# A ConvNeXt-V2 block on one core: squares ahead of norms, bn_stats of half means, and one convolution bank in three copied by VectorE in some slots

## The chip, the cores and the metric

The kernel runs on one core of one Trainium2 chip. A core has a matrix engine (TensorE, PE in the profile, with its weight loads as PEld), VectorE (DVE), ScalarE (ACT), GpSimd (POOL) and SyncE (SP, used here to issue DMA transfers). Each engine works through its own queue in order; semaphores hold an instruction until what it needs is there. TensorE writes into PSUM (8 banks of 128 partitions by 512 f32 values); the other tiles lie in SBUF; DRAM is reached by DMA. The metric is device time of the whole program in microseconds (us), smaller is better.

## The reference

The input is one image of 512 x 512 pixels with C = 96 channels in bf16; the hidden width is 4C = 384.

```python
for i in range(K):                       # K = 3: depthwise 3 x 3 convolution
    for j in range(K):
        out = out + xp[:, i:i+H, j:j+W, :] * dw[i, j][None, None, None, :]
h = _layernorm(out, axis=-1)             # over the 96 channels of a pixel, eps 1e-5
h = jnp.einsum('bhwc,ce->bhwe', h, w1)   # 96 -> 384
h = _gelu(h)
gx = jnp.sqrt((h * h).sum(axis=(1, 2), keepdims=True) + 1e-6)   # per channel, over all pixels
nx = gx / (gx.mean(axis=-1, keepdims=True) + 1e-6)
h = grn_gamma * (h * nx) + grn_beta + h
h = jnp.einsum('bhwe,ec->bhwc', h, w2)   # 384 -> 96
return x + h
```

The sum of h * h per channel needs every pixel before the second product can be scaled. So there are two phases: all pixels through convolution, norm, first product and GELU for the sums, and then all pixels again through the second product.

## The kernel before

The image is cut into 128 blocks of four rows (2048 pixels each). **Phase 1** is a loop over slots (line 832 on); slot s works on many blocks at once, each at its own stage. A table `at` says which stage of which block falls into which slot. For a block b in the steady part: its x rows are loaded by SP four slots ahead (`load_x`), turned by two VectorE transposes in slot b - 3 (`turn_x`), and convolved on TensorE in slot b (`conv_taps`), in three bursts of 24 matmuls into three PSUM banks, Y3. Each burst uses two of the banks: the first banks 0 and 1, the second 1 and 2, the third 2 and 0. `evac` (line 500) writes the three banks to the bf16 tile `y_bf` with one ScalarE instruction. In slot b + 1 GpSimd squares it (`stage_sq`, tile `ysq`); in slot b + 2 TensorE sums y and y^2 over channels (`stage_stats`, matmuls with `rowsel`), VectorE moves the sums of four blocks out of PSUM (`stage_moments`, tile `mom`), and over the next slots GpSimd makes 1/sigma of the four blocks (`stage_rstd` and `stage_newton`), VectorE transposes it (`rt`), SP writes it to DRAM and reads it back spread over partitions (`rbc`, about four slots later). In slot b + 10 GpSimd multiplies (`stage_norm`, tile `yn`), in b + 11 SP writes yn to DRAM and in b + 12 reads it back with channels on partitions (`ynT`), and in b + 14 the block goes through the first product and GELU (`mlp_units`).

Such a slot with a product has twelve PSUM banks of product, each turned to `g` by ScalarE's GELU: three instructions of 1024 columns and six of 512. The order in a slot is written out by hand in lines 894 to 924: convolution bursts (`conv`), products (`unit`), g^2 statistics (`squares`) and the sums of y (`stage_stats`) take turns. At the top of the slot (lines 833 to 850) stand SP's issues and GpSimd's work: `newton`, then `norm` of block s - 10 (line 845), then the square of block s - 1 (line 847), then `rstd`. SP's issues follow the same order in every slot: the x load, the ynT read, the write of yn, `rbc` or the rows of 1/sigma, a third of a stored g.

**The sums of g^2.** A part of g (`cm_quads(b)` of its four quarters: 4 for a block that is stored whole, b mod 10 in 0, 3, 7; 2 for the block behind such a one; 3 for the rest) has channels on partitions, and VectorE takes `bn_stats` of each 512 values of a channel (`entry`, tile `bst`). `bn_stats` gives six numbers: count, mean and count times variance of one half of the values (256), and the same of the other half. The remaining quarters go through TensorE (`gram`). A whole block's last three statistics are put off to the end of the next slot, so each slot has nine. Each 32 entries make a group; `aggregate` (line 774) reduces a group with three `bn_aggr`, one for each 128 channels, to mean and variance (`mv`), and `second_moments` (line 784) turns them into sums of squares (`parts`): once for all groups but the last in the last slot but one, and once for the last group behind the last slot. The chain from there to the scaled weights `W2s` stands ahead of phase 2.

From slot 128 on there is no convolution (`mlp_tail`): a drain in which the last blocks wait for norms. **Phase 2** then goes over all blocks with g held, stored or recomputed (`gr`), and writes the output.

In set-up, `Wd` lies in one of the five `g` buffers, before its first use; `dwx` is a constant tile of its own, and `npx` holds the number of values of each group.

Of the kernel before, what the change touches and what calls it, by code (L numbers as in the profile page):

```python
# [56 lines left out]
def kernel(  # L57
# [80 lines left out]
    dwx = consts.tile([9, NI, GR, 32], bf16, name="dwx")  # L138
# [17 lines left out]
    mv = consts.tile([128, NCH, NACC, 2], f32, name="mv")  # L156
    parts = consts.tile([128, NCH, NACC + 1], f32, name="parts")
    npx = consts.tile([128, NACC], f32, name="npx")
    grp = {}
    NYT = 6  # L160
    yn_ring = [prepool.tile([128, GR, W], bf16, name=f"ynT{i}") for i in range(NYT)]
# [25 lines left out]
    with ExitStack() as p1:  # L187
# [31 lines left out]
        def load_x(b):  # L219
# [15 lines left out]
                sp.dma_start(out=o, in_=i_)  # L235
            xins[b] = t

        Wd = gpool.tile([128, NQ, NCH, QW], bf16, name="g")[:].rearrange("p t j w -> p (t j w)")[
            :, :NI * 9 * 32].rearrange("p (i k c) -> p i k c", i=NI, k=9)
# [163 lines left out]
        n = 0  # L403
# [35 lines left out]

        def setup_rest():  # L440
            dve.memset(ones_f[:], 1.0)
            for k in range(NACC):
                dve.memset(npx[:, k:k + 1], float(GROUPS[k] * QW))
            dve.tensor_copy(out=gam[:], in_=gam_bf[:])

        def turn_x(b):
# [20 lines left out]
        def conv_taps(b, spare):  # L467
            if spare:
                Ua, Ub = banks(2), banks(1)
                Y = [Ua[:, 0, :], Ua[:, 1, :], Ub[:, 0, :]]  # L470
            else:
                Y = [Y3[:, i, :] for i in range(NI)]
            mms = []
            for n in range(3):
                mms.append([(h, j, (n + h) % NI, dx) for dx in (0, -1, 1) for j in range(GR) for h in range(2)])
            flat = [m for ms in mms for m in ms]
            first = {}
            last = {}
            for n, (h, j, i, dx) in enumerate(flat):
                first.setdefault((i, j), n)  # L480
                last[i, j] = n

            def burst(n, fence=True):
                k = sum(len(ms) for ms in mms[:n])
                for h, j, i, dx in mms[n]:
                    src = b + shift(h, j)
                    o0, o1 = max(0, -dx), W - max(0, dx)
                    pe.matmul(
                        Y[i][32 * j:32 * j + 32, o0:o1],
                        lhsT=Wq[64 * h:64 * h + 64, i, dx + 1, j, :],  # L490
                        rhs=x_rows(src, 64 * h, 64 * h + 64, i, MB * (1 + dx) + o0, o1 - o0)
                        if 0 <= src < NBLK else zrow[64 * h:64 * h + 64, o0:o1],
                        start=first[i, j] == k,
                        stop=last[i, j] == k,
                    )
                    k += 1
                if n < 2 and fence:
                    pe.drain()

            def evac():  # L500
                y = ypool.tile([128, NI, W], bf16, name="y_bf")
                if spare:
                    act.activation(out=y[:, 0:2, :], in_=Ua, func=ACTF.Identity)
                    act.activation(out=y[:, 2, :], in_=Ub[:, 0, :], func=ACTF.Identity)
                else:
                    act.activation(out=y[:], in_=Y3, func=ACTF.Identity)
                ybf[b] = y
# [270 lines left out]

        def combine(b):
            for k in sorted(bsts):  # L780
# [49 lines left out]
        for s in range(last_slot + 1):  # L830
# [11 lines left out]
            store_next()  # L842
            for k in get("newton"):
                stage_newton(k, pool)
            for b in get("norm"):
                stage_norm(b)
            for b in get("sqp"):
                stage_sq(b, False)
            for k in get("rstd"):
                stage_rstd(k, pool)  # L850
            mlp = get("mlp")
# [37 lines left out]
            else:  # L889
# [25 lines left out]
                unit(8, 2)  # L915
                unit(10, 1)
# [30 lines left out]
            if s == last_slot - 2:  # L947
                for n in range(PRE):
                    load_xr(n, sp)
            if s == last_slot - 1:  # L950
                for n in range(3):
                    stage_xb(ORDER[n], pool, B2bc_f)
                second_moments(0, NACC - 1)
            if s == last_slot:
                for n in range(PRE):
                    load_rest(n, sp, sp)
# [8 lines left out]
        dve.tensor_reduce(out=sums[:], in_=parts[:, :, :NACC], axis=AX.X, op=ALU.add)  # L965
        for j in range(NCH):
            junk = bstpool.tile([128, 128], f32, name="junk")
            dve.scalar_tensor_tensor(out=junk[:], in0=gram[:, j, :], scalar=1.0, in1=ident_f[:],
                                     op0=ALU.mult, op1=ALU.mult, accum_out=parts[:, j, NACC:NACC + 1])
        ssq = gsm.tile([128, NCH], f32, name="ssq")  # L970
        dve.scalar_tensor_tensor(out=ssq[:], in0=sums[:], scalar=GRN_EPS, in1=parts[:, :, NACC],
                                 op0=ALU.add, op1=ALU.add)
        gi = gsm.tile([128, NCH], i32, name="gi")
        dve.tensor_scalar(out=gi[:], in0=ssq[:].bitcast(i32), scalar1=-0.5, scalar2=float(0x5F3759DF),
# [84 lines left out]
```

## Time and profile before

| what | us |
|---|---|
| median of three runs (1481.1, 1482.73, 1484.31) | 1482.73 |
| the profiled execution's own time | 1478.75 |
| its span from first to last instruction | 1477.0 |
| busy: TensorE, VectorE, ScalarE, GpSimd | 1392.1, 1182.9, 1413.9, 1300.8 |
| g^2 statistics on VectorE (`bst<-g`, 1110) | 671.1 |
| evictions of y_bf on ScalarE (135) | 199.9 |
| norms (126) and squares (114) on GpSimd | 391.2 and 313.7 |
| aggregates of a full group on VectorE (33) | 30.4 |

All instructions issued through the kernel's in-order wrapper carry line 35, so groups are told apart by their tiles: `y_bf<-PS` is the eviction of a convolution, `g<-PS` a GELU, `bst<-g` a statistic, `mv<-bst` an aggregate, `xT<-xin` a transpose, `ysq<-y_bf` a square, `yn<-y_bf,rbc` a norm, and `PS<-rowsel,ysq` the sums of y^2 on TensorE. A line of the timeline gives the start, the length, the engine, the operation, the tiles, the shape and the number of instructions that stand together, and in brackets the idle time ahead of it and what ended that. Phase 1 ends near 972 us.

### The profile page before, as it was taken

The page shows a single profiled execution, that of the slowest core. Times are in us where ns is not written, and L with a number is a line of the kernel's source. Part 1 is how long each engine was busy: PE and PEld are TensorE (multiplying, and loading weights), DVE is VectorE, ACT ScalarE, POOL GpSimd, SP SyncE. Part 2 cuts the span into 40 slices and gives each one's busy share as a digit, 9 for nine tenths or more (in the row PEclk, how much of TensorE's full clock was granted, in tenths as well). Part 3 has the DMA queues.
Part 4 walks back from the last instruction along what each step waited for, and adds up shares of the span by engine and source line. Part 5 has one row for each costly group of instructions (what it writes and reads, how often), then busy time and mean ns, then how long its engine had stood idle before and what let it go on. Part 6 is the DMA issues. An engine that isn't in the chain of part 4 may idle for free.

```text
span 1477.0 us, 54487 instructions
## 1 busy us (share of the span) xinstructions
PE 1392.1 (94%) x23125; PEld 811.5 (55%) x23125; DVE 1182.9 (80%) x2135; ACT 1413.9 (96%) x1595; POOL 1300.8 (88%) x923
## 2 busy tenths in 40 slices
PE   7888989999999999999999998789999999999998
PEld 3343444444444444444444445467777767777766
DVE  7748989999999999999999987965555555555545
ACT  6888989999999999999999999999999999999987
POOL 2559899999999999999989988569999999999997
PEclk9999999999999999999999999999999999999999
DMA  6577788888878888888878866659999999999997
GB/s 180 164 218 240 236 248 268 258 264 255 282 236 262 269 268 257 277 245 272 261 245 270 271 212 191 201 193 364 367 327 386 397 379 398 404 392 406 387 373 306
DMA packets 167913, 422.03 MB, mean 286 GB/s; under 512 B 34326, under 2 KB 84182, under 8 KB 163190
## 3 DMA queue, kind: packets, MB, share of 16 engines
q1 hardware_dynamic: 151428, 314.98, 65.0%
q0 software_dynamic: 14880, 103.43, 18.6%
q8 instruction: 181, 2.97, 0.9%
q14 instruction: 62, 0.51, 0.1%
q10 hardware_dynamic: 1362, 0.15, 0.1%
HBM read 262.16 MB, written 156.22 MB: 283 GB/s over the span
## 4 chain that ended last, share of the span: by engine, by line
PE 28%; ACT 23%; POOL 19%; DMA 17%; issue 5%; SPq 5%; DVE 3%; POOLq 0%; ACTq 0%; DVEq 0%
PE PS L35 28%; ACT g L35 16%; POOL yn L35 6%; POOL xb L327 6%; ACT y_bf L35 5%; SPq L35 5%; POOL ysq L35 4%; DMA ynT<-yn_dram 4%; DMA out_dram<-o_sb 3%; DMA yn_dram<-yn 3%; DMA rbc<-r_dram 3%; DMA xin<-in_x_dram 2%; DVE bst L35 1%; DMA g_dram<-g 1%; ACT gr L35 1%
## 5 line engine op out<-in xcount | busy, mean ns | idle before, releaser
L35 ACT ACTIVATE g<-PS 128x512 bf16<-128x512 f32 (+2 forms) x1062 | 727.9, 868 | 15.3 <-PE PS L35 15.0
L35 DVE BATCH_NORM_STATS2 bst<-g 128x6 f32<-128x512 bf16 x1110 | 671.1, 674 | 35.4 <-ACT g L35 34.8
L35 ACT ACTIVATE gr<-PS 128x1536 bf16<-128x1536 f32 x360 | 498.1, 1458 | 17.5 <-PE PS L35 13.1
L35 POOL TENSOR_TENSOR yn<-y_bf,rbc 128x1536 bf16<-128x1536 bf16 x126 | 391.2, 3107 | 78.3 <-ACT rbc L35 24.1
L35 DVE TENSOR_TENSOR o_sb<-PS,xb 128x384 bf16<-128x384 f32 x512 | 278.4, 557 | 224.2 <-PE PS L35 189.9
L327 POOL TENSOR_TENSOR xb<-xr,B2c 128x1536 f32<-128x1536 bf16 x118 | 368.2, 3135 | 2.0 <-POOL xb L327 0.5
L35 PE MATMUL PS<-xT,Wq 64*32 64x511 bf16 (+1 forms) x9198 | 340.5, 389 | 26.2 <-ACT y_bf L35 9.2
L35 PE MATMUL PS<-ynT,w1p 128*128 128x512 bf16 x1161 | 335.1, 383 | 25.0 <-ACT g L35 5.4
L35 POOL TENSOR_TENSOR ysq<-y_bf 128x1536 bf16<-128x1536 bf16 x114 | 313.7, 2752 | 12.8 <-ACT y_bf L35 12.8
L35 PE MATMUL PS<-ynT,w1s 128*128 128x512 bf16 x1020 | 276.3, 380 | 0.0
L35 PEld LDWEIGHTS <-gr 128*128 128x128 bf16 x4296 | 212.5, 98 | 64.0 <-issue 6.0
L35 PE MATMUL PS<-W2s,gr 128*128 128x96 bf16 x4224 | 223.7, 206 | 4.8 <-DVE o_sb L35 4.6
L35 PEld LDWEIGHTS <-Wq 64*32 64x32 bf16 x9216 | 111.9, 90 | 193.3 <-issue 144.7
L35 ACT ACTIVATE y_bf<-PS 128x1536 bf16<-128x1536 f32 (+2 forms) x135 | 199.9, 1486 | 16.6 <-PE PS L35 12.1
L35 PEld LDWEIGHTS <-w1p 128*128 128x128 bf16 x1161 | 89.7, 98 | 183.0 <-issue 128.6
L35 DVE STREAM_TRANSPOSE xT<-xin 128x576 f32<-128x576 f32 (+1 forms) x256 | 181.7, 750 | 7.8 <-DMA xin<-in_x_dram 7.7
L35 PEld LDWEIGHTS <-g 128*128 128x128 bf16 x1704 | 104.8, 98 | 86.7 <-issue 54.8
L35 PE MATMUL PS<-w1p,ynT 128*128 128x256 bf16 (+2 forms) x822 | 125.2, 272 | 7.8 <-ACT xT L35 3.2
L35 PE MATMUL PS<-g 128*128 128x128 bf16 x1464 | 122.6, 220 | 2.8 <-DVE PS L35 2.5
L35 PEld LDWEIGHTS <-w1s 128*128 128x128 bf16 x1020 | 82.2, 98 | 40.8 <-issue 0.6
L35 PEld LDWEIGHTS <-gl 128*128 128x128 bf16 x1680 | 83.4, 98 | 28.4 <-issue 7.0
L35 PE MATMUL PS<-W2s,gl 128*128 128x96 bf16 x1680 | 90.3, 206 | 4.2 <-DVE o_sb L35 3.9
(108 smaller groups left out, 704.3 us busy)
## 6 DMA issues: line engine op xcount, KB each, us to landing
xin<-in_x_dram SPq DMA_DIRECT2D x126, 432.0 KB
g_dram<-g SPq DMA_DIRECT2D x105, 512.0 KB
gl<-g_dram POOLq DMA_DIRECT2D x35, 1536.0 KB, 10.5
yn_dram<-yn SPq DMA_DIRECT2D x512, 96.0 KB
ynT<-yn_dram SPq DMA_DIRECT2D x128, 384.0 KB
out_dram<-o_sb SPq DMA_DIRECT2D x127, 384.0 KB
xr<-in_x_dram POOLq DMA_DIRECT2D x123, 384.0 KB, 6.6
ynT<-yn_dram SPq DMA_DIRECT2D x255, 128.0 KB
```

The lines of the kernel that those rows point to most:

```text
L35: r = f(*a, **k)
L327: pq.tensor_tensor(out=xb[:], in0=grp[q]["xr"][:], in1=bias[:, None, :].to_broadcast([128, PXP, C]), op=ALU.add)
```

## The change

In words, part by part:

- In each slot GpSimd makes the square (`sqp`) ahead of the norm.
- `aggregate` takes, for each 128 channels, one `bn_stats` of the group's half means (twice the number of entries, up to 64 values, 24 bytes apart), and one reduction that adds the half variances (times count) of all three. `second_moments` has five operations where it had three, and its early call comes one slot earlier.
- In slots with a convolution whose product block has `cm_quads` of 2, ScalarE evicts banks 0 and 1 of the convolution and VectorE copies bank 2; there the third pair of statistics, `squares(2)`, stands behind that copy in VectorE's queue.
- `dwx` moves into the `g` buffer that holds `Wd`; `npx` and its memsets go; the sums of `gram`'s diagonal get a tile of their own.

```diff
+    mom2 = consts.tile([128, NCH, NACC, 2, 3], f32, name="mom2")
+    tot2 = consts.tile([128, NACC, NCH], f32, name="tot2")
+    parts = consts.tile([128, NCH, NACC, 2], f32, name="parts")
...
-            def evac():
+            def evac(shared=False):
                 y = ypool.tile([128, NI, W], bf16, name="y_bf")
-                if spare:
+                if shared:
+                    act.activation(out=y[:, 0:2, :], in_=Y3[:, 0:2, :], func=ACTF.Identity)
+                    dve.tensor_copy(out=y[:, 2, :], in_=Y3[:, 2, :])
+                elif spare:
...
         def aggregate(k):
             bst = bsts.pop(k)
+            n = 2 * GROUPS[k]
+            v = bst[:].rearrange("p j e (h s) -> p j (e h) s", h=2)[:, :, :n]
             for j in range(NCH):
-                dve.bn_aggr(out=mv[:, j, k, :], in_=bst[:, j, :GROUPS[k], :].rearrange("p a s -> p (a s)"))
+                dve.bn_stats(out=mom2[:, j, k].rearrange("p h s -> p (h s)"), in_=v[:, j, :, 1])
+            dve.tensor_reduce(out=tot2[:, k, :], in_=v[:, :, :, 2], axis=AX.X, op=ALU.add)
...
         def second_moments(k0, k1):
-            v, p = mv[:, :, k0:k1, :], parts[:, :, k0:k1]
-            dve.tensor_tensor(out=p, in0=v[:, :, :, 0], in1=v[:, :, :, 0], op=ALU.mult)
-            dve.tensor_tensor(out=p, in0=p, in1=v[:, :, :, 1], op=ALU.add)
-            dve.tensor_tensor(out=p, in0=p, in1=npx[:, None, k0:k1].to_broadcast([128, NCH, k1 - k0]), op=ALU.mult)
+            v, p = mom2[:, :, k0:k1], parts[:, :, k0:k1]
+            dve.tensor_tensor(out=p, in0=v[:, :, :, :, 1], in1=v[:, :, :, :, 1], op=ALU.mult)
+            dve.tensor_tensor(out=p, in0=p, in1=v[:, :, :, :, 0], op=ALU.mult)
+            dve.tensor_tensor(out=p, in0=p, in1=v[:, :, :, :, 2], op=ALU.add)
+            dve.tensor_scalar(out=p, in0=p, scalar1=float(QW // 2), scalar2=None, op0=ALU.mult)
+            dve.tensor_tensor(out=p[:, :, :, 0], in0=p[:, :, :, 0],
+                              in1=tot2[:, k0:k1, :].rearrange("p k j -> p j k"), op=ALU.add)
...
+            for b in get("sqp"):
+                stage_sq(b, False)
             for b in get("norm"):
                 stage_norm(b)
-            for b in get("sqp"):
-                stage_sq(b, False)
...
+                shared = evac is not None and cm_quads(b) == 2
                 unit(6, 1)
-                squares(2)
+                if not shared:
+                    squares(2)
                 unit(7, 1)
...
                 conv(2)
                 if evac:
-                    evac()
+                    evac(shared)
+                if shared:
+                    squares(2)
```

More of the change, by code (lines that the diff above doesn't have):

```diff
@@ L137 @@
     dw9 = consts.tile([9, C], bf16, name="dw9")
-    dwx = consts.tile([9, NI, GR, 32], bf16, name="dwx")
     eye32 = consts.tile([128, 32], bf16, name="eye32")
@@ L155 @@
     NACC = len(GROUPS)
-    mv = consts.tile([128, NCH, NACC, 2], f32, name="mv")
-    parts = consts.tile([128, NCH, NACC + 1], f32, name="parts")
-    npx = consts.tile([128, NACC], f32, name="npx")
+    mom2 = consts.tile([128, NCH, NACC, 2, 3], f32, name="mom2")
+    tot2 = consts.tile([128, NACC, NCH], f32, name="tot2")
+    parts = consts.tile([128, NCH, NACC, 2], f32, name="parts")
+    dsum = consts.tile([128, NCH], f32, name="dsum")
     grp = {}
@@ L236, in load_x @@
             xins[b] = t
-        Wd = gpool.tile([128, NQ, NCH, QW], bf16, name="g")[:].rearrange("p t j w -> p (t j w)")[
-            :, :NI * 9 * 32].rearrange("p (i k c) -> p i k c", i=NI, k=9)
+        g_setup = gpool.tile([128, NQ, NCH, QW], bf16, name="g")[:].rearrange("p t j w -> p (t j w)")
+        Wd = g_setup[:, :NI * 9 * 32].rearrange("p (i k c) -> p i k c", i=NI, k=9)
+        dwx = g_setup[:9, NI * 9 * 32:NI * 9 * 32 + NI * GR * 32].rearrange("p (i q c) -> p i q c", i=NI, q=GR)
         zrow = consts.tile([128, W], bf16, name="zrow")
@@ L441, in setup_rest @@
             dve.memset(ones_f[:], 1.0)
-            for k in range(NACC):
-                dve.memset(npx[:, k:k + 1], float(GROUPS[k] * QW))
             dve.tensor_copy(out=gam[:], in_=gam_bf[:])
@@ L949 @@
                     load_xr(n, sp)
+                second_moments(0, NACC - 1)
             if s == last_slot - 1:
@@ L952 @@
                     stage_xb(ORDER[n], pool, B2bc_f)
-                second_moments(0, NACC - 1)
             if s == last_slot:
@@ L964 @@
         sums = gsm.tile([128, NCH], f32, name="sums")
-        dve.tensor_reduce(out=sums[:], in_=parts[:, :, :NACC], axis=AX.X, op=ALU.add)
+        dve.tensor_reduce(out=sums[:], in_=parts[:].rearrange("p j k h -> p j (k h)"), axis=AX.X, op=ALU.add)
         for j in range(NCH):
@@ L968 @@
             dve.scalar_tensor_tensor(out=junk[:], in0=gram[:, j, :], scalar=1.0, in1=ident_f[:],
-                                     op0=ALU.mult, op1=ALU.mult, accum_out=parts[:, j, NACC:NACC + 1])
+                                     op0=ALU.mult, op1=ALU.mult, accum_out=dsum[:, j:j + 1])
         ssq = gsm.tile([128, NCH], f32, name="ssq")
-        dve.scalar_tensor_tensor(out=ssq[:], in0=sums[:], scalar=GRN_EPS, in1=parts[:, :, NACC],
+        dve.scalar_tensor_tensor(out=ssq[:], in0=sums[:], scalar=GRN_EPS, in1=dsum[:],
                                  op0=ALU.add, op1=ALU.add)
```

## The prediction, before the changed kernel was run

> **What bounds the kernel now.** First the page's part on busy time in 40 slices (about 37 us each; slices 7 to 23 are the steady part of phase 1):
>
> ```profile
> DVE  7748989999999999999999987965555555555545
> ACT  6888989999999999999999999999999999999987
> POOL 2559899999999999999989988569999999999997
> ```
>
> All are full in phase 1. The busy time by stretch says how full (columns: stretch, its us, then busy us of PE, PEld, DVE, ACT and POOL):
>
> ```profile
> 100.00:127.00 27.00, 20.81 (x342) 9.13 (x340) 19.76 (x33) 21.48 (x32) 19.58 (x18) 0.94 0.78 226
> 241.00:840.00 599.00, 576.58 (x10461) 283.41 (x10459) 596.60 (x1024) 598.67 (x852) 564.61 (x422) 1.00 0.84 262
> 883.00:900.00 17.00, 12.48 (x146) 8.38 (x143) 11.16 (x21) 13.04 (x12) 16.26 (x15) 0.90 0.59 185
> ```
>
> From 241 to 840 us ScalarE (ACT) and VectorE (DVE) both lack under 0.5% of being always busy, and VectorE's row of waits for this stretch is empty. ScalarE loses time in two places only, near 117 and near 890. Next, a slot in order of time:
>
> ```profile
> 410.14 1.57 ACT L35 ACTIVATE y_bf<-PS 128x1536 bf16<-128x1536 f32 x1
> 411.48 1.65 ACT L35 ACTIVATE g<-PS 128x1024 bf16<-128x1024 f32 x2
> ...
> 410.36 1.42 DVE L35 STREAM_TRANSPOSE xT<-xin 128x576 f32<-128x576 f32 x2
> 411.70 5.40 DVE L35 BATCH_NORM_STATS2 bst<-g 128x6 f32<-128x512 bf16 x9
> 417.01 1.42 DVE L35 STREAM_TRANSPOSE xT<-xin 128x576 f32<-128x576 f32 x2
> ...
> 411.24 0.38 PE L35 MATMUL PS<-w1p,ynT 128*128 128x128 bf16 x2
> 411.77 0.87 PE L35 MATMUL PS<-xT,Wq 64*32 64x512 bf16 x24 [0.15 <-ACT y_bf L35]
> ...
> 308.99 2.77 DVE L35 BATCH_NORM_AGGREGATE mv<-bst 128x2 f32<-128x192 f32 x3
> 311.68 1.22 DVE L35 BATCH_NORM_STATS2 bst<-g 128x6 f32<-128x512 bf16 x2
> ```
>
> Starts count, since neighbours overlap by some 0.08 us on VectorE and 0.2 us on ScalarE. ScalarE: y_bf 1.34 us (410.14 to 411.48), and a slot of about 7.04. VectorE: two transposes 1.34, nine statistics 5.31 (411.70 to 417.01, 0.59 each), so about 6.65, 0.15 for moments, and 2.69 for three aggregates about every 10.7 slots: 7.05. TensorE's next convolution burst starts 0.15 us late, on y_bf. Last, the two stalls:
>
> ```profile
> 114.09 3.09 POOL L35 TENSOR_TENSOR yn<-y_bf,rbc 128x1536 bf16<-128x1536 bf16 x1
> 117.14 2.75 POOL L35 TENSOR_TENSOR ysq<-y_bf 128x1536 bf16<-128x1536 bf16 x1
> ...
> 119.94 0.46 PE L35 MATMUL PS<-rowsel,ysq 128*128 128x4 bf16 x12 [4.62 <-POOL ysq L35]
> 122.37 1.46 PE L35 MATMUL PS<-ynT,w1p 128*128 128x512 bf16 x3
> 124.57 0.82 PE L35 MATMUL PS<-ynT,w1p 128*128 128x512 bf16 x3
> ...
> 892.23 0.46 PE L35 MATMUL PS<-rowsel,ysq 128*128 128x4 bf16 x12 [2.23 <-POOL ysq L35]
> ```
>
> At both places TensorE stands still for a square that GpSimd (POOL) makes behind a norm.
>
> **Squares in front of norms.** GpSimd's work is the same; each square comes 3.05 us earlier (117.14 less 114.09), each norm 2.75 later. At 119.94 the wait falls from 4.62 to 1.57: -3.05 us, all on the path, since ScalarE idles there. Between 241 and 840 nothing waits long for squares: 0. At 892 up to -2.5 us (2.23, and 0.3 at 898) is to be had, but a later norm is queued in front of everything SP does: the write of yn waits for it, and behind the write stand the store of g, the reload of rbc, the next x load and the next ynT read. Cover: in the steady part ynT reads are issued 10 to 17 us ahead of use and land in about 5, and x loads land at least 3.4 us before their transposes, mostly 5 to 10; 2.75 fits. In the drain reads are issued about 8 us ahead and land in 3 to 5, so 2.75 and the 2.5 gained use up the 3 to 5 that are spare. I take -0.7 there (ends -2.5 and +1), and +0.5 for x loads that come late in the batches with least room (0 to +3).
>
> **Half means on VectorE.** Between 241 and 840 there are 25 aggregates at 0.90: 22.4 us go. In their place 25 bn_stats of 64 values and 8.3 reductions of 192. No row shows either. A statistic of 512 starts 0.59 before the next; 448 values less at 1.04 ns (a VectorE column: 557 ns at 384 columns of o_sb against 279 at 128 of mom is 1.09, 0.59 over 512 less a start-up is about 1) leaves 0.125; bounds 0.07 (a memset of 128) and 0.2. A reduction of 39 takes 0.19, so one of 192 some 0.35, started 0.27 before the next; bounds 0.1 and 0.9 (the aggregate that read the same 192). Sum 3.1 + 2.3 = 5.4 us, between 2.6 and 12.5.
>
> **A third of y_bf on VectorE.** By the schedule 35 slots share, 25 of them between 241 and 840. ScalarE saves 512 columns: 1.34 less the 0.90 that a 1024 takes, 0.43 us; TensorE passes on at most 0.3 of it, because its last unit (411.24 and 0.22 for two) leaves 411.46 as the earliest start of the burst that now begins at 411.77. The copy on VectorE is bounded by the cast of 512 f32 in SBUF (0.43 long, 0.35 apart) and by 557 ns scaled from 384 to 512 (0.74). Two o_sb additions in a row stand 0.51 apart, also out of PSUM; with 128 columns more that is 0.64, which I take, as the nearest row. 25 x 0.64 = 16 us, between 8.7 and 18.6.
>
> [...]
>
> VectorE's balance between 241 and 840: -22.4 + 5.4 + 16.0 = -1.0 us, with ends -11 and +9. ScalarE could give 25 x 0.3 = 7.5, but VectorE has no free time, and it may no longer fall behind: bank 2 of the convolution is needed by the next slot's second burst, some 3.1 us after y_bf begins, and the copy ends 3.2 us behind the transposes' start (1.34 transposes, 1.18 two squares, 0.68 copy). So VectorE paces this stretch, and -1.0 is what arrives. Behind the copy in VectorE's queue wait squares(2) and all later statistics; who waits for those is only the g buffers, slots away. In slots 17 to 27 VectorE has room (27% of 100:127 is idle): 4 x 0.3 = -1.2. In slot 6 VectorE is on the chain that leads to the first rstd: +0.6.
>
> **The rest.** Behind the last statistics three aggregates (0.57) become three small bn_stats and a reduction (about 0.4), and three dependent additions at 0.2 become five: +0.3, on the path to W2s. The earlier part of second_moments lies where VectorE waits for ScalarE; dwx in g and dropped memsets cost nothing, they are set-up. Phase 2 (505 us) is untouched.
>
> **Sum.** -3.05 - 0.7 + 0.5 - 1.0 - 1.2 + 0.6 + 0.3 = -4.5 us on the profiled 1478.75. That execution is 4.0 below the median of 1482.73; on the median, 1478.2.
>
> [...]
>
> **Rivals.** (1) The copy is cheap, 0.35: 7.2 us less on VectorE, until TensorE's 7.5 binds: 1471.7. For it: the cast's row; against: every PSUM row. Chance 0.10. (2) The drain pays in full and x loads are never late (-1.8 and -0.5): 1475.9. For it: GpSimd waits 2.66 us for rbc at 876, room for a square. 0.12. (3) Slower: VectorE's new work costs more than it frees. Place: the saturated stretch, where each 0.1 us on a copy is 2.5 us, and a stride of 24 bytes under the statistics has no row. At the upper ends +9 in place of -1.0: 1488. It decides from +3.5 on the balance (copy 0.82, or reduction 0.8), where the forecast's gain is gone. 0.25, of which 0.05 ends within 0.2%. (4) Later norms eat the gain: SP falls behind, x loads and ynT reads come late, and the 4.5 us are given back: 1482.7. 0.10, half same, half slower.
>
> **The numbers.** Forecast 0.43, own range 1474.5 to 1481.5. What a measurement tells from no change is 0.2%, 3 us: of the forecast 0.32 is faster, 0.11 same. Faster 0.32 + 0.10 + 0.12 = 0.54; same 0.11 + 0.05 + 0.05 = 0.21; slower 0.20 + 0.05 = 0.25. The range 1471 to 1488 leaves out the best part of (1) and the worst of (3), some 0.15.
>
> **What would show it.** The wait at 119.94 about 1.6; none at 892; VectorE's busy time between 241 and 840 still full, while ScalarE's falls by about 9 us with small idle pieces put down to PE; the copy 0.68 long. Wrong if VectorE begins to idle (rival 1), if its balance is over +3.5, or if transposes wait for x or TensorE for ynT.

## The result and the profile after

The changed kernel takes 1476.22 us (median of 22 runs, 1467.0 to 1484.89) beside 1481.6 us for the kernel before in the same set of runs: ratio 0.9964, 95% interval 0.9951 to 0.9977. In a second set (first row of the experiments) it was 0.9973, 0.9953 to 0.9993. So it is faster by 0.3 to 0.4%, where -4.5 us (0.3%) was forecast. The profiled execution of the changed kernel has an own time of 1477.4 us and a span of 1475.6, against 1478.75 and 1477.0 before.

Runs of one kernel in one set spread over 10 to 20 us, and one run of the kernel with norms first, of 2616 us, is left out of its ratio. A difference between two single profiles is therefore read only where a wait or an instruction names it.

The busy time in 40 slices, changed kernel:

```profile
DVE  8849989999899999999999997965555555555555
ACT  7889999999899999999998999999999999999997
POOL 3469989998899999999999998379999999999998
```

ScalarE is no longer at 9 throughout the middle: its eleventh digit, from 369 us on, is an 8. By stretch (stretch, its us, busy us of PE, PEld, DVE, ACT, POOL, granted clock, DMA share, GB/s):

```profile
100.00:127.00 27.00, 23.94 (x415) 11.48 (x414) 23.07 (x40) 25.07 (x37) 22.92 (x19) 1.00 0.69 197
241.00:840.00 599.00, 572.08 (x10254) 278.90 (x10261) 585.72 (x1035) 580.94 (x834) 557.27 (x420) 0.99 0.85 259
883.00:900.00 17.00, 14.83 (x226) 9.71 (x225) 13.61 (x24) 16.52 (x19) 16.09 (x18) 1.00 0.61 177
```

Two stretches gained: ScalarE has 25.07 busy us of 27 in place of 21.48, and 16.52 of 17 in place of 13.04. The middle lost. ScalarE's busy time falls by 17.7 us, and VectorE's, forecast as still full, by 10.9. Since the stretch is as long as before, both are idle for that much longer. For the same work, from the eviction of block 37 to that of block 121, ScalarE's busy time falls by 5.4 us only (591.5 to 586.1), about half of 25 times 0.43: the evictions take 10.6 us less, but the GELUs of 512 columns overlap less (0.506 us from start to start, before 0.496, with mean lengths of 0.681 and 0.711) and take 4.9 more. Its idle time there rises from 0.1 to 17.8 us.

The early stall, in order of time:

```profile
113.56 0.46 PE L35 MATMUL PS<-rowsel,ysq 128*128 128x4 bf16 x12 [1.29 <-POOL ysq L35]
```

The wait of 4.62 us is 1.29; the one of 2.23 at 892 is gone. In the middle there is a new one (idle time and its releaser in brackets):

```profile
368.03 3.11 POOL L35 TENSOR_TENSOR yn<-y_bf,rbc 128x1536 bf16<-128x1536 bf16 x1 [3.23 <-DMA xin<-in_x_dram]
375.33 0.32 POOL L35 TENSOR_TENSOR rstd<-nt,rn 128x64 bf16<-128x64 f32 x1
375.69 0.25 DVE L35 STREAM_TRANSPOSE rt<-rstd 128x64 bf16<-128x64 bf16 x1 [2.93 <-POOL rstd L35]
375.85 0.65 DVE L35 CAST y_bf<-PS 128x512 bf16<-128x512 f32 x1
376.56 1.28 PE L35 MATMUL PS<-xT,Wq 64*32 64x512 bf16 x23 [4.30 <-DVE y_bf L35]
378.42 0.60 ACT L35 ACTIVATE g<-PS 128x512 bf16<-128x512 f32 x1 [5.10 <-PE PS L35]
```

Slot 55 has both a copy and a transpose `rt`. GpSimd's norm starts 3.23 us late, so 1/sigma, which stands behind it in GpSimd's queue, is late, so `rt` waits 2.93 us in VectorE's queue. (The x load in the bracket is no input of the norm; what the norm waited for is open.) The copy of bank 2 stands behind `rt`. TensorE waits 4.30 us for the copy, and ScalarE 5.10 for TensorE. TensorE's granted clock is 0.50 from 377 to 380 us, right behind this wait. At 806 (slot 115) the same costs ScalarE 3.43. Over the whole stretch from 241 to 840 us these waits add up to (us in total, times, longest):

```profile
PE PS L35 <- DVE y_bf L35: 10.3, 10, 4.3
ACT g L35 <- PE PS L35: 14.3, 13, 5.1
```

The new instructions by group (count, busy us, mean ns):

```profile
L35 DVE CAST y_bf<-PS 128x512 bf16<-128x512 f32 x35 | 23.5, 670 | 0.0
L35 DVE BATCH_NORM_STATS2 mom<-bst 128x6 f32<-128x64 f32 x33 | 5.8, 229 | 0.0
L35 DVE TENSOR_REDUCE tot<-bst 128x3 f32<-128x192 f32 x11 | 4.4, 398 | 0.0
```

Start to start they stand 0.588, 0.148 and 0.315 us apart. The end of phase 1, ahead of W2s:

```profile
958.68 9.27 POOL L35 TENSOR_TENSOR xb<-xr,B2bc_f 128x1536 f32<-128x1536 bf16 x3 [15.28 <-DMA xr<-in_x_dram]
965.96 2.02 DVE L35 TENSOR_TENSOR parts<-mom 128x6 f32<-128x6 f32 x1
968.01 0.37 DVE L35 TENSOR_TENSOR parts<-parts,mom 128x6 f32<-128x6 f32 x2
```

A product of six numbers takes 2.02 us, and it ends (967.98) where GpSimd's last xb addition ends (967.95). The products behind it take 0.18 each.

Where the time went, as starts of evictions (`y_bf` of blocks 20, 37, 121 and 127), end of W2s and end of the span, in us. "Products" is the sum of the first three products (before: of its three operations) of the early call of second_moments:

| run | ratio, 95% interval | 20 | 37 | 121 | 127 | W2s | span | products |
|---|---|---|---|---|---|---|---|---|
| before | 1 | 127.3 | 248.2 | 839.8 | 882.0 | 971.7 | 1477.0 | 0.58 |
| changed | 0.9964 (0.9951 to 0.9977) | 119.6 | 241.4 | 845.3 | 886.8 | 974.0 | 1475.6 | 0.79 |
| changed, again | 0.9973 (0.9953 to 0.9993) | 121.9 | 242.2 | 838.8 | 881.0 | 970.1 | 1472.3 | 0.79 |
| squares first alone | 1.0021 (0.9998 to 1.0045) | 118.8 | 241.3 | 836.9 | 882.8 | 973.2 | 1478.1 | 4.69 |
| no copies | 0.9992 (0.9961 to 1.0023) | 125.1 | 243.6 | 836.7 | 880.7 | 970.7 | 1473.2 | 0.79 |
| norms first | 1.0039 (1.0012 to 1.0065) | 127.3 | 245.4 | 842.5 | 887.4 | 984.1 | 1486.8 | 8.34 |
| half means alone | 1.0062 (1.0037 to 1.0087) | 127.7 | 246.2 | 840.2 | 882.3 | 981.0 | 1486.6 | 8.46 |
| half means gated | 0.9984 (0.9957 to 1.0012) | 125.9 | 244.9 | 846.6 | 891.7 | 982.1 | 1484.6 | 0.79 |
| rt behind copy | 0.9974 (0.9945 to 1.0004) | 123.6 | 243.9 | 836.3 | 878.5 | 965.1 | 1466.4 | 0.81 |
| no copy in turn slots | 0.9989 (0.9968 to 1.001) | 122.9 | 244.3 | 839.6 | 882.5 | 970.4 | 1472.4 | 0.81 |
| bank 1 copied early | 1.0478 (1.0453 to 1.0503) | 126.0 | 256.3 | 907.5 | 952.8 | 1046.7 | 1549.1 | 8.07 |
| bank 2 done early | 0.9995 (0.9971 to 1.0019) | 123.3 | 245.5 | 842.7 | 885.1 | 978.9 | 1481.2 | 8.09 |
| the same, half shared | 1.0005 (0.9986 to 1.0025) | 123.4 | 242.8 | 848.0 | 891.0 | 978.3 | 1480.1 | 0.81 |
| copy first, gated | 0.998 (0.9962 to 0.9998) | 126.6 | 246.9 | 844.8 | 889.2 | 981.0 | 1482.3 | 0.80 |

In the profiled pair the changed kernel is 6.8 us ahead at block 37, loses 12.3 to block 121, wins 0.7 to block 127 and 2.5 from there to W2s, and 3.6 in phase 2: -1.4 in all, as the spans say. In its second profile the figures are -6.0, +5.0, 0, -0.6 and -3.0.

Two rows show how far such figures can be trusted. Half means alone and half means gated run the same instructions between blocks 37 and 121, and took 594.0 and 601.7 us for them: 7.7 us, or 0.09 us a slot, apart in single profiles. And the lead at block 37 is not all due to the squares: the changed kernel is 4.1 us ahead at block 10 already (66.8 against 70.9 us), ahead of the stall, and 1.68 us of that is a wait of TensorE for `ynT` at 31.4 us that the changed kernel's profile hasn't. From block 16 to block 20, the stretch with the stall, it gains 3.2 us (30.6 against 33.8).

### The profile page after: what moved, and what is told of

Read it like the earlier page. It is cut to its first block, busy times and chain, and to the rows that moved or that the text cites. A ratio compares the mean times of both kernels' runs of the same rounds, so it can differ in the third digit from the quotient of the medians.

```text
span 1475.6 us, 54538 instructions
## 1 busy us (share of the span) xinstructions
PE 1394.1 (94%) x23125; PEld 810.0 (55%) x23125; DVE 1183.4 (80%) x2174; ACT 1405.9 (95%) x1595; POOL 1300.9 (88%) x923
## 4 chain that ended last, share of the span: by engine, by line
POOL 31%; PE 22%; ACT 13%; DVE 12%; DMA 11%; issue 7%; SPq 3%; POOLq 0%; ACTq 0%; DVEq 0%
PE PS L35 22%; POOL xb L328 17%; ACT g L35 8%; DVE bst L35 8%; POOL yn L35 7%; DMA xin<-in_x_dram 3%; ACT y_bf L35 3%; SPq L35 3%; DMA ynT<-yn_dram 3%; POOL xr L283 2%; DMA rbc<-r_dram 2%; DVE xT L35 2%; DMA yn_dram<-yn 2%; POOL ysq L35 1%; POOL var L35 1%
## 5 line engine op out<-in xcount | busy, mean ns | idle before, releaser
L35 ACT ACTIVATE g<-PS 128x512 bf16<-128x512 f32 (+2 forms) x1062 | 730.7, 842 | 26.0 <-PE PS L35 22.4
L35 PE MATMUL PS<-xT,Wq 64*32 64x511 bf16 (+1 forms) x9198 | 347.6, 388 | 29.2 <-DVE y_bf L35 11.7
L35 ACT ACTIVATE y_bf<-PS 128x1536 bf16<-128x1536 f32 (+2 forms) x135 | 181.7, 1351 | 15.7 <-PE PS L35 10.6
L35 DVE STREAM_TRANSPOSE xT<-xin 128x576 f32<-128x576 f32 (+1 forms) x256 | 181.4, 748 | 12.8 <-DMA xin<-in_x_dram 10.6
L35 PEld LDWEIGHTS <-w1p 128*128 128x128 bf16 x1161 | 89.8, 98 | 180.3 <-issue 123.3
L35 PEld LDWEIGHTS <-g 128*128 128x128 bf16 (+1 forms) x1707 | 105.5, 98 | 89.1 <-issue 57.0
## 6 DMA issues: line engine op xcount, KB each, us to landing
gl<-g_dram POOLq DMA_DIRECT2D x35, 1536.0 KB, 10.7
```

The source lines that it names most:

```text
L35: r = f(*a, **k)
```

## The experiments

**The changed kernel again**, beside other kernels of its set. The edit is none.

> The changed kernel as it is, so that it stands beside the others in one set of runs: ratio 0.995 to 0.998, with waits of rt for rstd ahead of copies and ScalarE stalls behind them, in the slots that have both.

Ratio 0.9973, as expected. Its longest ScalarE wait in the middle is 1.7 us, though, where the first profile had 5.10 and 3.43: the same queue, but GpSimd happened to be less late. Its waits for TensorE sum up to 8.2 us in 14 places, nearly all behind slots with a copy.

**Squares first alone.**

```diff
+            for b in get("sqp"):
+                stage_sq(b, False)
             for b in get("norm"):
                 stage_norm(b)
-            for b in get("sqp"):
-                stage_sq(b, False)
```

> The kernel before with one edit: in each slot GpSimd makes the square ahead of the norm. Theory (the squares pay at both stalls and cost nothing between): the wait for ysq at 119.94 falls from 4.62 to about 1.6 and the one at 892 goes, so 4 to 6 us less than before, ratio 0.996 to 0.9973. Rival (norms that come later make SP, the reload of rbc and the x loads late, and that gives the gain back): ratio 0.999 to 1.001, with longer waits for rbc and for x between 241 and 840 us.

The outcome is the rival's, the reason neither's. The kernel is as far ahead at block 37 as the changed one (7.0 us), yet the ratio is 1.0021, and its interval reaches from 0.9998 to 1.0045: no gain. GpSimd waits longer for rbc in the middle, as the rival had it (7.4 us, before 2.9), but that isn't where ScalarE loses. In its profile the gain goes in two places. One is blocks 58, 90 and 122, whose slots last 8.50, 10.44 and 10.73 us; this is 90:

```profile
607.58 2.77 DVE L35 BATCH_NORM_AGGREGATE mv<-bst 128x2 f32<-128x192 f32 x3
615.09 0.28 DVE L35 TENSOR_SCALAR mom<-PS 128x128 f32<-128x128 f32 x1
615.68 0.80 PE L35 MATMUL PS<-g 128*128 128x128 bf16 x6 [2.19 <-DVE PS L35]
616.95 1.08 ACT L35 ACTIVATE g<-PS 128x512 bf16<-128x512 f32 x2 [2.20 <-PE PS L35]
```

`gram` and the sums S lie in one PSUM bank. `gram`'s next products wait until VectorE has taken the moments out and cleared S, and VectorE gets to that late, because three aggregates stand a slot ahead of it. Before, the same place cost TensorE 0.46 us: there the moments come 4.9 us behind the eviction's start (614.11 to 619.00), here 6.6 (608.47 to 615.09). The likely reason is that ScalarE had gained time at the first stall, and VectorE, which was full, had not followed. That would make the half means belong to the squares, since they take 2.77 us of aggregates out of that queue. The kernel with both and without copies (next) fits this: its longest wait at these places is 1.14 us (here 2.44), and the three slots take 7.50, 7.91 and 8.00 us. But its ratio does not prove it. The other place is the early call of second_moments, which in this kernel and before comes a slot later than in the changed one. Its three operations take 4.69 us, before 0.58, and behind them ScalarE idles 3.79 us up to 973.35, a gap that before hasn't; why they are slow is told under half means alone.

**No copies** (squares first and half means).

```diff
-                shared = evac is not None and cm_quads(b) == 2
+                shared = False
```

> The changed kernel with ScalarE evicting all three banks in every slot: squares first and half means, no copies. Theory (the copies buy nothing in the middle and cost two stalls of some 4 to 5 us there): VectorE has 15 us of room between 241 and 840, ScalarE paces slots at 7.04 us, no stall near 378 and 806; 2 to 6 us less than the changed kernel, ratio to before 0.992 to 0.995. Rival (the copies carry part of the gain): slower than the changed kernel by 1 us or more, ratio to before 0.997 or above.

The theory's gain did not come: its range of 0.992 to 0.995 lies outside the interval, 0.9961 to 1.0023. The rival's claim, that the copies carry part of the gain, isn't shown either, since the interval takes in the changed kernel's ratios. The profile is clear on the mechanism. VectorE's waits between 241 and 840 us:

```profile
DVE rt L35 <- POOL rstd L35: 8.4, 9, 2.1
DVE xT L35 <- PE PS L35: 3.9, 5, 1.3
DVE xT L35 <- DMA xin<-in_x_dram: 3.4, 3, 1.5
```

and ScalarE's:

```profile
ACT g L35 <- PE PS L35: 0.6, 1, 0.6
```

VectorE stands still for 15.7 us, longer than in the changed kernel (11.0), and ScalarE waits 0.8 us in all. What makes VectorE's waits cost ScalarE time is the copy, because TensorE waits for it.

**Norms first** (half means and copies).

```diff
-            for b in get("sqp"):
-                stage_sq(b, False)
             for b in get("norm"):
                 stage_norm(b)
+            for b in get("sqp"):
+                stage_sq(b, False)
```

> The changed kernel with the norm ahead of the square again: half means and copies alone. Theory A (the order of squares and norms is what pays at 119.94 and 892): the 4.62 and 2.2 us stalls are back and the time is 3 to 6 us over the changed kernel. On the two stalls in the middle: if norms that come later make rstd late (theory B), the waits of rt for rstd fall back to before's 8.6 us in all and the stalls near 378 and 806 go, which gives up to 9 us back, so the time is equal to or below the changed kernel; if the copy alone makes them (rival), they stay and the ratio to before is 0.999 to 1.002.

Ratio 1.0039: slower than before, where the changed kernel is at 0.9964. On the waits theory A holds (block 20 at 127.3, as before; waits for squares of up to 5.5 us are back). Theory B holds for the two big stalls only (ScalarE's longest wait in the middle is 1.0), but in their place TensorE waits there for squares, 10.2 us in 13 places. Behind the last block it loses a further 7 us, which neither theory had; the next run shows why. The ratio is 0.0075 over the changed kernel's, about 11 us; without these 7 some 4 us would be left, which lies in theory A's range of 3 to 6. That is an estimate from one profile, and no run separates the two.

**Half means alone.** The kernel has `aggregate` and `second_moments` of the changed one, norms first, and `shared = False` as above.

> The kernel before with the half means alone (norms ahead of squares, ScalarE evicts all banks). Theory: ScalarE is as full as VectorE between 241 and 840 us, so VectorE's freed 16 us only become idle time; the stalls near 117 and 892 stay; 0 to 2 us less than before, ratio 0.9985 to 1.000. Rival (VectorE's lag is what sets the pace in the middle, and its aggregates delay the moments): 3 to 6 us less, ratio 0.996 to 0.998.

Ratio 1.0062, outside both. The middle is as forecast (37 to 121 in 594.0 us, before 591.6), but from block 127 to W2s it takes 98.6 us where before took 89.7:

```profile
955.53 9.33 POOL L35 TENSOR_TENSOR xb<-xr,B2bc_f 128x1536 f32<-128x1536 bf16 x3 [16.65 <-DVE bst L35]
...
956.29 0.28 DVE L35 TENSOR_REDUCE tot<-bst 128x3 f32<-128x108 f32 x1
956.49 2.29 DVE L35 TENSOR_TENSOR parts<-mom 128x72 f32<-128x72 f32 x1
958.81 6.17 DVE L35 TENSOR_TENSOR parts<-parts,mom 128x72 f32<-128x72 f32 x2
```

Three products of 72 numbers take 8.46 us; in the changed kernel the same three took 0.79 (0.24 and 0.55). While GpSimd makes three xb additions of 3.1 us, each product lasts until about where one of these ends (the last product to 964.98, the third addition to 964.86). The reduction and the small `bn_stats` in the same microseconds, with one input, take their usual time (0.28 and 0.19 us; 0.27 and 0.19 in the changed kernel, where no addition runs beside them).

**Half means gated**, the run that tests this.

```diff
                 second_moments(0, NACC - 1)
+                dve.tensor_copy(out=B2d[:], in_=B2bc_f[:])
...
-                    stage_xb(ORDER[n], pool, B2bc_f)
+                    stage_xb(ORDER[n], pool, B2d)
```

> Half means alone, as in the run of that name, with one wait more: GpSimd's first three xb additions read a copy of the bias that VectorE makes behind the early call of second_moments, so these no longer run beside each other. Theory (a VectorE tensor_tensor with both inputs in SBUF stands still until the GpSimd addition beside it ends): the products of 2.29 and 3.08 us fall to 0.25 to 0.28, W2s comes 7 to 8.5 us earlier after the last block's eviction, and the time falls by 6 to 9 us against half means alone, ratio to before 0.998 to 1.002. Rival (half means alone are slow for another reason, late squares or the drain): the products stay long or the time stays at a ratio of 1.004 or above.

```profile
964.85 0.24 DVE L35 TENSOR_TENSOR parts<-mom 128x72 f32<-128x72 f32 x1
965.13 0.55 DVE L35 TENSOR_TENSOR parts<-parts,mom 128x72 f32<-128x72 f32 x2
```

The theory holds: 0.79 us in place of 8.46, the last eviction to W2s 90.4 us in place of 98.6, and the ratio goes from 1.0062 to 0.9984, with intervals that don't touch, though the two runs stood in different sets. The products meet the additions in each of the four profiles with the changed `second_moments` in which xb begins ahead of them, by 1.0 to 1.3 us, and in none in which it begins behind them, by 2.3 to 3.5 (gated 1.7 and 3.2); the changed kernel has 3.3 and 3.5. In the old place, behind twelve more statistics, squares first alone is caught too (xb from 955.47 to 964.75, the operations from 960.26 on), and before escaped by 0.13 us (xb ends at 962.71, the first operation starts at 962.84).

**rt behind the copy.**

```diff
+                if not shared:
+                    for k in get("turn"):
+                        stage_turn(k)
                 conv(2)
...
                 if shared:
                     squares(2)
+                    for k in get("turn"):
+                        stage_turn(k)
```

> The changed kernel with one move: in the slots with a copy, the transpose rt stands behind the copy and behind squares(2) in VectorE's queue instead of ahead of the copy. Theory (the copy is held up by rt, which waits for GpSimd's rstd): TensorE's waits for VectorE's y_bf fall from 11.7 us to under 3, ScalarE's stalls of 5.10 and 3.43 go, 6 to 10 us less than the changed kernel, ratio to before 0.990 to 0.993. Rival (VectorE's bill paces the middle whatever stands in its queue): 0 to 2 us less than the changed kernel.

The mechanism holds, the size doesn't. TensorE's waits for the copy between 241 and 840 fall from 10.3 us (5.7 in the second profile) to 3.3, and ScalarE's from 14.3 (8.2) to 5.0, the longest 1.3. The mean slot from block 37 to 121 falls from 7.19 (7.10) to 7.05, which is not clear of what one program's profiles differ by. And 0.9974 is no better than the changed kernel's own ratios.

**No copy in turn slots.**

```diff
-                shared = evac is not None and cm_quads(b) == 2
+                shared = evac is not None and cm_quads(b) == 2 and not get("turn")
```

> The changed kernel without a copy in the five slots (35, 55, 75, 95, 115) that also have a transpose rt; 30 slots still share. Theory (only the copy behind a waiting rt stalls): no ScalarE stall over 1.5 us between 241 and 840, 5 to 9 us less than the changed kernel, ratio to before 0.991 to 0.994. Rival (VectorE is behind in every shared slot, and a late copy stalls wherever it stands): stalls move to other shared slots and at most 2 us are gained.

The edit took the copy out of a sixth slot too, 27. No stall is over 1.5 us, as the theory had it, but the gain is the rival's: ScalarE still waits 6.4 us for TensorE in 12 places, up to 1.1 each and mostly behind other slots with a copy, and the ratio is 0.9989. A waiting rt is the worst case of a late copy, not the only one.

**Bank 1 copied early.**

```diff
+            def copy_1():
+                y = ypool.tile([128, NI, W], bf16, name="y_bf")
+                early.append(y)
+                dve.tensor_copy(out=y[:, 1, :], in_=Y3[:, 1, :])
...
-                    act.activation(out=y[:, 0:2, :], in_=Y3[:, 0:2, :], func=ACTF.Identity)
-                    dve.tensor_copy(out=y[:, 2, :], in_=Y3[:, 2, :])
+                    y = early.pop()
+                    act.activation(out=y[:, 0:3:2, :], in_=Y3[:, 0:3:2, :], func=ACTF.Identity)
...
                 squares(1)
+                if shared:
+                    copy_1()
...
-                if not shared:
-                    squares(2)
+                squares(2)
```

> The changed kernel with VectorE copying bank 1 in place of bank 2, right behind squares(1): bank 1 is complete after the second burst, half a slot earlier, and the next slot writes it only in its first burst, behind ScalarE's eviction of banks 0 and 2. The copy then stands ahead of rt. Theory (the copy's deadline, not its price, costs the middle): TensorE's waits for VectorE's y_bf fall to under 1 us, mean slot between blocks 37 and 121 under 7.02 us (changed kernel 7.19), 10 to 15 us less than the changed kernel, ratio to before 0.987 to 0.991. Rival (VectorE's bill sets the middle): mean slot 7.05 or more and no less than the kernel with rt behind the copy, ratio 0.995 or above.

A miss: ratio 1.0478. ScalarE's waits in the middle:

```profile
ACT y_bf L35 <- DVE y_bf L35: 39.8, 24, 1.8
```

In 24 of 25 shared slots ScalarE's own eviction waits for VectorE's copy. The likely reason, which wasn't tested by itself, is that banks 0 and 2 of the tile are written by one instruction, whose span holds bank 1; in the next run, where that instruction writes banks 0 and 1 and VectorE copies bank 2, ScalarE has no such wait between 241 and 840 us. So the run did not test the deadline. It prices the opposite: with the copy ahead of the eviction, the two slots around a shared eviction grow from 14.0 to some 16.8 us.

**Bank 2 done early**, the same idea without that order.

```diff
-                mms.append([(h, j, (n + h) % NI, dx) for dx in (0, -1, 1) for j in range(GR) for h in range(2)])
+                mms.append([(h, j, (0, 2, 1)[(n + h) % NI], dx) for dx in (0, -1, 1) for j in range(GR) for h in range(2)])
...
+            def copy_2():
+                y = ypool.tile([128, NI, W], bf16, name="y_bf")
+                early.append(y)
+                dve.tensor_copy(out=y[:, 2, :], in_=Y3[:, 2, :])
...
                 squares(1)
+                if shared:
+                    copy_2()
```

> The changed kernel with the order of the convolution's banks changed so that bank 2 (VectorE's) is complete after the second burst and banks 0 and 1 (ScalarE's) after the third; VectorE copies bank 2 behind squares(1), ahead of squares(2) and rt, and no instruction waits for a neighbour's bank. Theory (the copy's deadline, one burst of the next slot, is what stalls ScalarE, not its price): TensorE's waits for VectorE's y_bf fall from some 6 us to under 1, ScalarE's waits between 241 and 840 from 8 us to under 3, the mean slot to 6.98 to 7.03, 5 to 9 us less than the changed kernel, ratio to before 0.990 to 0.994. Rival (VectorE's bill: it has 597 us of work in these 599 us): mean slot 7.04 or more, ratio 0.996 or above.

```profile
425.25 0.67 DVE L35 CAST y_bf<-PS 128x512 bf16<-128x512 f32 x1
425.56 1.28 PE L35 MATMUL PS<-xT,Wq 64*32 64x512 bf16 x24
427.63 1.51 ACT L35 ACTIVATE g<-PS 128x1024 bf16<-128x1024 f32 x2 [0.46 <-ACT g L35]
```

The forecast fails, but the run did not give the copy more time either. Bank 2 is ready earlier, but it is also needed earlier, by the next slot's first burst, which begins at 425.56, while VectorE copies until 425.92; the burst takes 1.28 us (0.87 elsewhere) and ScalarE idles 0.46 us, which is what the smaller eviction had saved. Such a gap follows each of the 25 copies between 241 and 840, and the mean slot is 7.11. In the profiled execution the products also met xb (8.09 us); in how many of the other eleven runs they did is not known, so the ratio of 0.9995 can't be put down to the copy alone.

**The same, half shared.**

```diff
-                shared = evac is not None and cm_quads(b) == 2
+                shared = (evac is not None and cm_quads(b) == 2
+                          and not get("turn") and not get("moments"))
```

> The run with bank 2 complete early, with copies only in slots that have neither a transpose rt nor moments: about half of the shared slots. ScalarE then saves some 5 us between 241 and 840 in place of 10.7, and VectorE has some 8 us of room. Theory (two engines near their limit; best where both have room): VectorE idle for 5 to 10 us of these 599, ScalarE's waits under 2 us, mean slot 6.97 to 7.01, ratio to before 0.989 to 0.993, at or below the run that shares in all such slots. Rival (GpSimd with SP, or TensorE, sets the pace below 7.04): mean slot 7.03 to 7.06, ratio 0.995 to 0.998.

Ratio 1.0005, mean slot 7.21. Copies are left in 23 of the 35 slots. VectorE has room now (581 busy us of 599), and the copies are still late: TensorE waits 9.7 us for them. Five of these waits, of 1.3 to 2.1 us, cost ScalarE 11.4 us. Ahead of three of them (at 467, 612 and 757 us) VectorE had waited within the last 10 us, for x or for rstd. Ahead of the other two (395 and 829 us) it had not waited for 16 us and was simply behind with its work. So both play a part: VectorE's load around a copy, and its waits for GpSimd and the DMA queues, which its queue passes on to TensorE.

**Copy first, gated**: rt and squares(1) stand behind the copy, and the additions are gated as in half means gated. The move of rt and the gate are those of the runs above; the third move is this:

```diff
-                squares(1)
+                if not shared:
+                    squares(1)
...
                 if shared:
+                    squares(1)
                     squares(2)
```

> The changed kernel with three moves: in slots with a copy, the transpose rt and squares(1) as well stand behind the copy in VectorE's queue (ahead of it only squares(0) and the x transposes), and GpSimd's first three xb additions wait for the early call of second_moments. Theory (a copy stalls ScalarE by as much as VectorE is behind when it gets to it, so 1.2 us less ahead of it takes most stalls away; and products of second_moments never meet xb): ScalarE's waits between 241 and 840 under 3 us, mean slot 6.99 to 7.04, no product of 72 values over 0.6 us for two, W2s some 87 us after the last eviction; ratio to before 0.990 to 0.994. Rival (VectorE has no room, so its lag grows until the copy is late again whatever stands ahead of it): ScalarE's waits 5 us or more, mean slot 7.05 to 7.1, ratio 0.996 to 0.999.

Each side is half right. The copy is in time: there is no wait for VectorE's y_bf left in the middle. TensorE's waits there are now these:

```profile
PE PS L35 <- DVE PS L35: 12.1, 17, 1.6
```

TensorE waits in 17 places at the next thing that VectorE hands over, the cleared S; the likely reason is that it is no longer held at the copy and runs further ahead of VectorE. ScalarE's waits add up to 7.8 us, where the theory had under 3. The median slot behind a copy falls to 6.88 us (changed kernel 7.10), the others' rises from 6.99 to 7.06, and the mean is 7.12. The gate did its work (products 0.80).

No version was shown to be faster than the changed kernel: rt behind the copy comes nearest, with the best single profile, 1466.4.

## Why the prediction was right, and where it was wrong

The time and the sign were right; the sum behind them was right at the two stalls and wrong in the middle and at the end of phase 1. That the total came out near the forecast is in part luck. In the profiled pair the middle, put at -1.0, is 12.3 us slower, and the 7.8 us lead at block 20, the 2.5 us up to W2s and the 3.6 us of phase 2, most of which no term of the sum stands for, pay for it. Two of the prediction's own signs of being wrong came true: between 241 and 840 us VectorE is idle (it waits 11.0 us, though the copy isn't cheap), and transposes wait for x.

- **Squares in front of norms, -3.05 early.** Right in its place and size: the wait went from 4.62 to 1.29 us (1.57 was forecast), and ScalarE's two gaps behind it, 3.51 and 1.96, became one of 0.94. From block 16 to 20 the two profiles of the changed kernel gain 3.2 and 2.5 us. All the same the gain is less sure than one pair makes it look: this stretch takes 27.5 to 34.6 us in the ten profiles with squares first and 32.1 to 34.6 in the four with norms first. In the first profile TensorE's granted clock was 1.00 from 100 to 127 us (before 0.94, with 0.62 from 121 to 124.5), so a part of the gain may be the clock, for which the prediction's sum has no term; in the second it was 0.94 there too. What the prediction missed is that this gain isn't kept by itself: squares first alone gives it back at VectorE's moments.
- **Drain, -0.7.** The wait at 892 is gone and that stretch gained; from block 127 to W2s the two profiles of the changed kernel differ from before by -2.5 and -0.6, the loss at W2s included. The size was taken between ends and stays unsettled. The prediction also said that ScalarE loses time near 117 and 890 only. The trace of before has a third place, where it idles 2.07 us at 189 and 2.42 us at 195; the change leaves it as it is (2.04 and 2.68).
- **x loads and later norms, +0.5 and rival 4.** The late norms show: GpSimd's waits for rbc in the middle rise from 2.9 to 10.7 us, and transposes wait for x 2.2 us (before none). The price as such is small. What it sets off is the next point.
- **VectorE's balance, -1.0.** The bill was right: 25 aggregates of 0.90 go (-22.4); 25 statistics at 0.148 and 8.3 reductions at 0.315 come (6.3, forecast 5.4), 25 copies at 0.588 (14.7, forecast 16.0): -1.4. A copy was put at 0.64 from start to start, after the o_sb additions, and at 0.68 long; the trace has 0.588 and 0.670. But the step "so VectorE paces this stretch, and -1.0 is what arrives" failed: blocks 37 to 121 took 12.3 and 5.0 us longer. In the first profile that is ScalarE's 5.4 us less of work and 17.7 more of idleness. The two profiles of half means differ by 7.7 us in the same stretch, so the size is uncertain; the waits for the copy are in both profiles. The prediction had asked who waits for what stands behind the copy in VectorE's queue. Of what stands in front of it, it counted transposes and two statistics by their length alone, with no wait in them, and left out rt, which waits for GpSimd. It had noted the copy's deadline, 3.1 us after y_bf begins, and that the copy ends at 3.2, and then treated a missed deadline as pace instead of as a stall.
- **-1.2 in slots 17 to 27, +0.6 in slot 6.** No profile shows either: block 20 to 37 took 121.8 and 120.4 us, before 120.9.
- **The chain to W2s, +0.3.** It cost +1.84 us in the profiled pair: from the end of the last statistic to the first W2s instruction 7.69 us (965.71 to 973.40), before 5.85 (965.27 to 971.12), all of it the product of 2.02 us that waits for xb. That the earlier part costs nothing held, by a margin of 3.3 us; half means alone paid 8 there. And its move by a slot, costed at nothing, may be worth something once squares come first: in the old place squares first alone paid 4.1 in its profile.
- **"Phase 2 is untouched."** The two profiles have 501.7 and 502.3 us, before 505.3. Squares first alone and half means alone have 504.9 and 505.6, all others 501.3 to 502.7, and half means gated, with the same phase 2 as half means alone, 502.5. Before has a ScalarE wait of 2.76 us near 1429 that the changed kernel hasn't. What decides it stays open; it wasn't forecast and isn't claimed for the change.

So one part of the gain in the profiled pair is the forecast one, at the stall; the middle took back as much or more, and the rest came from where nothing had been expected, without a cause that the runs show. What the experiments show of the measured 0.3 to 0.4% is this: no kernel with only one or two of the three parts is shown to be faster than before (squares first alone 1.0021, half means gated 0.9984, half means with copies 1.0039, squares first with half means 0.9992). Only kernels with all three are, and the share of each part, of the copies above all, is open.

## What to carry to other kernels

Before a full engine takes over work that another engine waits for, read its queue ahead of the new instruction, with every wait in it: without copies VectorE stood still for 15.7 us here and ScalarE waited 0.8, while with a copy behind it one wait of 2.93 us became 4.30 of TensorE's and 5.10 of ScalarE's. VectorE's lag showed at more than one hand-over: when the copy was put first, TensorE waited 12.1 us in 17 places at the next one. And where two engines each do an edit's small operations next to a long one, look whether they overlap in time: here a margin of 3.3 us decided over some 8.

## What the runs showed of the hardware

A VectorE `tensor_tensor` with both inputs in SBUF lasted until a GpSimd addition beside it ended: with half means alone 2.29 us for one product of 72 numbers and 6.17 for the next two, in place of 0.24 and 0.55 (changed kernel), and 1.0 to 2.3 us for a product of six numbers in seven profiles, the changed kernel's two among them, against 0.17 (half means alone). In each of these cases the addition had begun first. A reduction beside one took 0.28 us, 0.27 without. What makes the two differ no run shows.

TensorE's granted clock was below 1 behind some short waits. In the changed kernel it was 0.50 from 377 to 380 us, behind a wait of 4.30 us; in the run of squares first alone 0.50 from 615.5 to 618.5, behind one of 2.19; and with bank 1 copied early 0.65 from 501 to 504.5, behind one of 1.47. In the second of the three, a run each of `gram`, first products and convolution took 0.80, 1.06 and 1.48 us there in place of 0.50, 0.59 and 0.87, so a stall of 2 us cost an estimated 1.4 more of TensorE's time. Behind a wait of 1.29 us (changed kernel, 113.56) the clock was 1.00 from 113.5 to 118 us. What decides between the two no run here settles.
